# A reordered plan of 1325 calls in an attention and PReLU-FFN kernel, with three operations moved to other engines

## The chip, the cores and the metric

The kernel runs on one core of a Trainium2 chip. The metric is the device time of one execution in microseconds (us), and the number given for a kernel is the median of several executions. The engines are TensorE (PE in the profile, with its weight loads shown apart as PEld), VectorE (DVE), ScalarE (ACT), GpSimd (POOL) and SyncE (SP, which only issues DMAs here).

## What is computed

Attention with normalised queries and keys feeds a two-layer network with a PReLU between the layers. q, k and v are (8, 12, 448, 64): batch, heads, sequence, head size. The weights of the network are 768 x 2048 and 2048 x 768, and alpha has 2048 slopes.

```python
q_n, k_n = rmsnorm(q, g_q), rmsnorm(k, g_k)     # x / sqrt(mean(x*x) + 1e-6) * g
attn = softmax(q_n @ k_n.T / sqrt(64))          # 448 x 448 for each of 8 x 12 heads
x = (attn @ v), heads side by side              # 3584 x 768
h = x @ w_in                                    # 3584 x 2048
g = maximum(h, 0) + alpha * minimum(h, 0)
out = g @ w_out                                 # 3584 x 768, float32
```

## The kernel before

**Tiles.** The 96 heads are worked in 24 groups y of four heads; three groups make a batch b (0 to 7). The hidden layer is worked in 16 blocks ft of 128 columns for each batch. The output has 28 tiles of 128 rows, in two halves of 384 columns (OH). Tiles 0 to 5 are plain products (`down`). From tile 6 on, tiles go in pairs, and each pair is made from seven half-depth products instead of eight (`qa1` to `qc2`, and `quad` for the pairs 22, 24 and 26), with sums of weight blocks made beforehand (`mix_weights`) and sums of activations made for each pair (`mix_two` for two of them, then `mix_rest` for the other two).

**The plan.** One string, `PLAN`, names 1325 calls in one total order, and a loop at the end of the kernel carries them out in that order. The schedule is manual: each engine runs the instructions that it gets in the order in which the plan issues them, and waits by semaphores for what other engines have to deliver. So the plan sets the order within each engine. A call that changes its place only against calls of other engines changes nothing.

```python
for step in PLAN.split():
    ...
    acts[name](*given)
```

**A group's path.** `load_qk` (issued on SP) brings q and k. `square` (L370 on POOL, L368 on ACT) and `reduce` (L392, L401 on DVE) form the sums of squares, `fold` adds them up, `root` (L422, L423 on ACT) takes the inverse root, `scale` (L430 for groups from 9 on, L442 for earlier ones; on POOL from group 4 on unless an engine is named) applies it. `turn` transposes on PE (L568) up to group 8; after that `flip` (DVE) does, and `weigh` (L549, ACT) applies the gains. `score` (L596, PE) fills a PSUM tile with scores, `soft` (L610, ACT) takes the exponential. `den`, or `den_pre` with two copies on DVE, and `attend` (L621, PE) are the sums over keys; `log` or `log_pre` (L669) and `invert` (L679) on ACT turn the denominators over, and `times` (L717, DVE) writes the normalised result, xT.

**A block's path.** `up` (L734, PE) computes hT; `slope` (L775 on ACT, or L770 on DVE where the plan says `vec`) writes alpha * h and `larger` (L781, DVE) the maximum of the two, gT. `down` (L801) and `down_end` (L812, a copy on DVE and a store), or the products (L863) with their additions on DVE (`qa1v` at L879, `qa2v` L887, `qb1v` L905, `qc1v` L926, `quad`'s own around L996), end it. `mix_weights` is L831, `mix_two` L851 and L852, `mix_rest` L859: on POOL, save for one piece of `mix_weights`, (2,3), on DVE.

**What a product or score waits for.** Its data, and a PSUM tile. The pools are small: two tiles `sc` and one `acc` of two banks each, and two tiles `mm` of one bank. A further argument of `score`, `up`, `down`, `den`, `attend` or of a product chooses the pool, so a PE call often waits until ACT or DVE has read out the tile that it gets. In SBUF, three buffers hold the exponentials (`expT`); `mix_two(22)` takes one of these for its sums, `mix_two(20)` three of the four `nat` buffers of loaded q and k.

Of the kernel before, what the change touches and what calls it, by code (L numbers as in the profile page):

```python
# [39 lines left out]
invert(0+1) score(2,1,0) score(2,3,1) scale(3,q) load_w_in(2,4,8) soft(2,6) soft(2,2) times(0+1,1,0)  # L40
soft(2,1) times(0+1,1,1) soft(2,3) square(4,k) score(2,5,0) soft(2,5) square(5,k,act) times(0+1,0,0)
turn(3) den(2,1) attend(2,0,1) score(3,0,1) log(2) reduce(4,k,None) load_w_out(2) score(3,1,0)
square(4,q) load_w_in(3,0,4) invert(2) soft(3,1) begin(1) soft(3,0) times(2,0,0) begin(0)
square(5,q,act) up(0,0,0) reduce(4,q,None) up(0,1,0) slope(0,0) slope(0,1,vec) load_qk(6) root(4)
begin(3) begin(2) scale(4,q) score(3,5,0) up(0,4,0) larger(0,0) reduce(5,k) larger(0,1)
load_w_out(0) load_qk(7) reduce(5,q) slope(0,4) up(0,2,0) larger(0,4) slope(0,3) slope(0,2)
up(0,5,0) larger(0,3) scale(4,k) up(0,6,0) slope(0,5,vec) load_w_out(1) score(3,2,0) soft(3,5)
score(3,3,0) larger(0,2) square(6,q) slope(0,6) soft(3,3) soft(3,2) larger(0,5) turn(4) up(0,8,0)
score(4,0,1) soft(4,0) score(4,3,0) up(0,3,1) larger(0,6) score(4,1,0) soft(4,3) up(0,9,0) up(0,7,1)
up(0,11,0) slope(0,8,vec) square(6,k) larger(0,8) root(5) score(3,4,0) score(4,6,0) slope(0,9)  # L50
scale(5,k) reduce(6,q) up(0,13,0) larger(0,9) soft(4,1) slope(0,7) scale(5,q) soft(3,4)
slope(0,11,vec) larger(0,11) up(0,10,0) larger(0,7) square(7,q) soft(4,6) up(0,12,1) score(3,6,0)
slope(0,13) slope(0,10,vec) score(4,2,0) load_v(1) slope(0,12) larger(0,10) soft(4,2) larger(0,13)
up(0,14,0) larger(0,12) reduce(6,k) square(7,k,act) turn(5) slope(0,14) up(0,15,0) score(5,4,1)
soft(3,6) load_qk(8) root(6) larger(0,14) slope(0,15,vec) reduce(7,k) score(4,4,0) score(5,2,0)
larger(0,15) soft(5,4) scale(6,q,vec) down(1,0,0) soft(5,2) score(4,5,0) soft(4,4) soft(4,5)
scale(6,k,vec) load_w_out(3) score(5,0,1) square(8,q,act) reduce(7,q) soft(5,0) score(5,1,0)
down(0,0,0) reduce(8,q) square(8,k,act) turn(6) den(3+4,1) attend(3+4,0,0) score(5,5,0) score(5,6,0)
soft(5,1) mix_weights(0,1) log(3+4) invert(3+4) soft(5,5) soft(5,6) mix_weights(0,3) attend(3+4,1,0)
score(6,0,1) score(5,3,0) soft(6,0) score(6,4,0) down_end(0,0) down(2,0,0) soft(5,3) root(7)  # L60
scale(7,q) load_qk(9) soft(6,4) scale(7,k) den(5,0) attend(5,0,1) down_end(1,0) mix_weights(0,2)
times(3+4,0,0) times(3+4,1,0) times(3+4,1,1) load_qk(10) log(5) down(0,1,0) reduce(8,k) invert(5)
down_end(2,0) times(5,0,1) times(5,0,0) times(5,0,3) times(5,0,2) score(6,5,1) mix_weights(0,0)
score(6,1,0) down_end(0,1) score(6,6,0) soft(6,5) turn(7) up(1,1,1) square(9,q) down(1,1,0) root(8)
reduce(9,q) soft(6,6) score(6,3,1) score(7,0,0) slope(1,1) score(6,2,0) up(1,2,0) up(1,0,0)
soft(6,1) soft(7,0) soft(6,3) square(9,k) up(1,3,1) up(1,4,0) slope(1,2) slope(1,0) larger(1,1)
down_end(1,1) reduce(9,k) root(9) larger(1,2) load_qk(11) larger(1,0) slope(1,3) scale(8,q)
soft(6,2) up(1,7,0) slope(1,4) larger(1,3) larger(1,4) scale(8,k) score(7,4,0) slope(1,7)
larger(1,7) up(1,5,1) scale(9,q) turn(8) score(7,5,0) soft(7,4) score(7,1,0) up(1,6,0) square(10,q)
slope(1,5) larger(1,5) up(1,10,0) soft(7,5) soft(7,1) up(1,8,1) scale(9,k) up(1,9,0) reduce(10,q)  # L70
score(7,2,0) slope(1,6) slope(1,10) larger(1,6) mix_weights(1,1) score(7,6,0) slope(1,8) slope(1,9)
soft(7,6) up(1,12,1) up(1,11,0) soft(7,2) square(10,k) up(1,13,0) larger(1,8) larger(1,10)
slope(1,12) score(7,3,0) larger(1,9) up(1,14,1) slope(1,11) slope(1,13) mix_weights(1,3)
reduce(10,k) up(1,15,0) load_v(2) soft(7,3) larger(1,12) load_qk(12) score(8,3,0) score(8,0,0)
den(6+7,0) slope(1,14) fold(10) root(10) slope(1,15) soft(8,0) down(2,1,0) larger(1,11) larger(1,13)
square(11,q) log(6+7) score(8,1,0) score(8,4,0) soft(8,3) flip(9,k) scale(10,q) larger(1,14)
larger(1,15) score(8,5,1) mix_weights(3,1) down_end(2,1) reduce(11,q) square(11,k) weigh(9)
soft(8,5) down(3,0,0) soft(8,1) scale(10,k) score(8,2,0) flip(9,q) reduce(11,k) score(8,6,0)
soft(8,4) fold(11) load_qk(13) attend(6+7,0,0) attend(6+7,1,0) score(9,1,0) score(9,0,0)
down_end(3,0) soft(8,2) invert(6+7) score(9,2,1) down(3,1,0) times(6+7,0,0) soft(8,6) root(11)  # L80
times(6+7,1,0) load_qk(14) flip(10,q) down(4,0,1) mix_weights(1,2) soft(9,0) times(6+7,1,1)
score(9,5,0) square(12,q) soft(9,1) soft(9,2) scale(11,q) score(9,3,0) square(12,k) reduce(12,q)
down_end(3,1) soft(9,5) mix_weights(3,2) flip(10,k) scale(11,k) down_end(4,0) den_pre(8)
reduce(12,k) soft(9,3) attend(8,0,0) log_pre(8) score(9,6,0) fold(12) invert(8) root(12)
score(9,4,0) weigh(10) times(8,0,3) down(5,1,0) soft(9,4) times(8,0,1) times(8,0,0) flip(11,q)
down(4,1,0) score(10,0,0) soft(9,6) score(10,3,1) down_end(5,1) times(8,0,2) soft(10,0) soft(10,3)
score(10,2,0) up(2,0,0) up(2,1,0) slope(2,0) score(10,6,0) score(10,1,1) up(2,7,0) up(2,2,0)
down_end(4,1) up(2,4,1) slope(2,1) flip(11,k) soft(10,2) soft(10,1) slope(2,7) up(2,3,0)
mix_weights(2,0) slope(2,2) larger(2,0) scale(12,q) soft(10,6) slope(2,4) up(2,6,0) scale(12,k)
up(2,8,1) larger(2,1) slope(2,3) mix_weights(2,3) mix_weights(1,0) larger(2,7) square(13,k)  # L90
larger(2,2) up(2,10,0) square(13,q) up(2,5,0) larger(2,4) weigh(11) up(2,12,1) larger(2,3)
slope(2,6) up(2,14,0) slope(2,8) reduce(13,q) score(10,5,0) slope(2,10) mix_weights(2,2) load_v(3)
slope(2,5) slope(2,12) slope(2,14) score(10,4,0) soft(10,4) square(14,q) up(2,9,1) up(2,13,0)
soft(10,5) slope(2,13) larger(2,6) larger(2,8) larger(2,10) reduce(13,k) up(2,11,0) larger(2,5)
larger(2,12) load_qk(15) score(11,0,0) fold(13) den(9+10,1) slope(2,11) mix_weights(3,3) qa1(6,0)
up(2,15,0) qa2(6,1) root(13) mix_weights(3,0) flip(12,q) slope(2,9) larger(2,14) larger(2,13)
down(5,0,0) log(9+10) slope(2,15) larger(2,11) larger(2,9) invert(9+10) soft(11,0) square(14,k)
flip(12,k) reduce(14,q) weigh(12) qa1v(6) larger(2,15) mix_weights(2,1) scale(13,q) score(11,3,1)
scale(13,k) score(11,4,0) attend(9+10,0,1) mix_two(6,pool) soft(11,4) qa2v(6) mix_rest(6)
score(11,1,0) down_end(5,0) times(9+10,0,0) soft(11,3) square(15,q) reduce(14,k) attend(9+10,1,0)  # L100
score(12,0,0) soft(11,1) times(9+10,1,0) score(11,2,0) qa3(6,1) qb1(6,0) soft(11,2) fold(14) qa3v(6)
score(11,5,0) times(9+10,1,1) score(11,6,1) score(12,1,0) soft(12,0) soft(11,6) qb2(6,0) qc1(6,1)
qb1v(6) score(12,3,0) flip(13,k) soft(11,5) qb2v(6) qc1v(6) soft(12,1) den_pre(11) root(14)
soft(12,3) flip(13,q) score(12,2,1) attend(11,0,1) soft(12,2) mix_two(8,pool) score(12,6,1) qa1(8,0)
scale(14,q) log_pre(11) qc2(6,0) invert(11) times(11,0,0) qa2(8,1) weigh(13) times(11,0,3) qa3(8,0)
# [1007 lines left out]
```

## Time and profile before

| what | before |
|---|---|
| median of 3 runs | 407.5 us (407.3, 407.5, 408.99) |
| profiled execution | 407.36 us |
| its span | 405.6 us |
| mean granted TensorE clock | 0.99 |
| POOL, ACT, DVE busy | 70%, 68%, 67% of the span |
| DMA packets | 37173, 58.39 MB |

In the rows, L and a number is the line of the kernel; a row gives the operation, the tile written <- the tiles read, and partitions x elements with the type. In views in order of time a row begins with its start and its duration in us, "x4" counts like instructions that follow one another, and a bracket at the end gives the idle time of the engine just before and what ended it. In views by group the two numbers behind the bar are the busy time in us and the mean duration of one in ns.

### The profile page before, as it was taken

The page shows a single profiled execution, that of the slowest core. Times are in us where ns is not written, and L with a number is a line of the kernel's source. Part 1 is how long each engine was busy: PE and PEld are TensorE (multiplying, and loading weights), DVE is VectorE, ACT ScalarE, POOL GpSimd, SP SyncE. Part 2 cuts the span into 40 slices and gives each one's busy share as a digit, 9 for nine tenths or more (in the row PEclk, how much of TensorE's full clock was granted, in tenths as well). Part 3 has the DMA queues.
Part 4 walks back from the last instruction along what each step waited for, and adds up shares of the span by engine and source line. Part 5 has one row for each costly group of instructions (what it writes and reads, how often), then busy time and mean ns, then how long its engine had stood idle before and what let it go on. Part 6 is the DMA issues. An engine that isn't in the chain of part 4 may idle for free.

```text
span 405.6 us, 11966 instructions
## 1 busy us (share of the span) xinstructions
PE 390.8 (96%) x5071; PEld 208.5 (51%) x5071; DVE 271.6 (67%) x486; ACT 274.3 (68%) x409; POOL 283.3 (70%) x187
## 2 busy tenths in 40 slices
...
GB/s 273 222 263 237 222 252 118 236 209 169 110 163 174 183 162 145 104 187 187 229 121 91 128 229 167 143 220 108 114 41 137 11 3 22 60 79 0 31 108 98
DMA packets 37173, 58.39 MB, mean 144 GB/s; under 512 B 4720, under 2 KB 28928, under 8 KB 37120
## 3 DMA queue, kind: packets, MB, share of 16 engines
...
q8 instruction: 39, 0.64, 0.6%
...
## 4 chain that ended last, share of the span: by engine, by line
PE 89%; DVE 3%; ACT 2%; DMA 2%; POOL 1%; issue 1%; SPq 1%; POOLq 0%; DVEq 0%
PE hT L734 25%; PE hTa L734 10%; PE sc L596 8%; PE op L801 7%; PE qx L863 5%; PE av L621 5%; PE qz L863 4%; PE qc L863 4%; PE oq L863 4%; PE qxa L863 3%; PE dn L621 2%; PE avb L621 2%; DMA arena<-in_k_dram 2%; PE oqm L863 2%; PE qza L863 1%; PE oqa L863 1%
## 5 line engine op out<-in xcount | busy, mean ns | idle before, releaser
L610 ACT ACTIVATE expT<-sc 128x896 f16<-128x896 f32 x168 | 146.2, 916 | 41.5 <-PE sc L596 39.8
L734 PE MATMUL hT<-xT,w_in_sb 128*128 128x448 f16 x552 | 114.7, 353 | 0.5 <-DVE xT L717 0.5
L734 PEld LDWEIGHTS <-w_in_sb 128*128 128x128 f16 x768 | 73.1, 98 | 73.4 <-issue 8.7
L430 POOL TENSOR_TENSOR qs<-nat,rr 128x896 f16<-128x896 f32 x30 | 65.6, 2218 | 24.2 <-ACT rr L423 21.1
L781 DVE TENSOR_TENSOR gT<-hT,gT 128x448 f16<-128x448 f32 x92 | 56.7, 620 | 35.6 <-ACT gT L775 34.9
L775 ACT ACTIVATE gT<-hT,cols 128x448 f16<-128x448 f32 x86 | 54.5, 634 | 36.8 <-PE hT L734 35.8
L370 POOL TENSOR_TENSOR nat<-nat 128x896 f32<-128x896 f32 (+1 forms) x38 | 62.5, 1652 | 11.4 <-DVE gT L781 6.1
L596 PE MATMUL sc<-qT,kT 64*32 64x448 f16 (+1 forms) x1092 | 50.0, 359 | 5.7 <-ACT expT L610 4.2
L863 PEld LDWEIGHTS <-gT 128*128 128x128 f16 x352 | 33.4, 98 | 25.5 <-issue 3.8
L734 PE MATMUL hTa<-xT,w_in_sb 128*128 128x448 f16 x204 | 44.2, 353 | 0.0
L717 DVE TENSOR_TENSOR xT<-av,rden 64x448 f16<-64x448 f32 (+1 forms) x37 | 27.2, 736 | 11.7 <-ACT rden L679 4.6
L596 PEld LDWEIGHTS <-kT 64*32 64x32 f16 (+1 forms) x1092 | 16.8, 94 | 33.9 <-issue 25.7
L851 POOL TENSOR_TENSOR gs<-gT 128x1024 f16<-128x1024 f16 x4 | 8.5, 2124 | 36.7 <-DVE gT L781 36.7
L392 DVE TENSOR_REDUCE sp<-nat 128x28 f32<-128x896 f32 x30 | 32.1, 1070 | 2.0 <-DMA nat<-in_k_dram 2.0
L801 PE MATMUL op<-w_out_sb,gT 128*128 128x384 f16 x176 | 30.3, 326 | 0.2 <-DVE xT L717 0.2
L775 ACT ACTIVATE gT<-hTa,cols 128x448 f16<-128x448 f32 x34 | 21.6, 635 | 12.0 <-PE hTa L734 11.5
L781 DVE TENSOR_TENSOR gT<-hTa,gT 128x448 f16<-128x448 f32 x34 | 21.1, 619 | 10.6 <-ACT gT L775 10.2
L801 PEld LDWEIGHTS <-gT 128*128 128x128 f16 x192 | 18.3, 98 | 14.5 <-issue 3.0
L621 PEld LDWEIGHTS <-vt 64*32 64x32 f16 x1344 | 19.5, 92 | 12.0 <-issue 2.1
L621 PE MATMUL av<-expT,vt 64*32 64x448 f16 x896 | 24.3, 350 | 0.0
L859 POOL TENSOR_TENSOR gT<-gT 128x1024 f16<-128x1024 f16 x11 | 23.5, 2132 | 0.0
L863 PEld LDWEIGHTS <-arena 128*128 128x128 f16 x136 | 12.7, 98 | 10.5 <-issue 2.3
(151 smaller groups left out, 548.2 us busy)
## 6 DMA issues: line engine op xcount, KB each, us to landing
...
```

Of the source, the lines that this page charges most:

```text
L370: (eng or nc.gpsimd).tensor_mul(out=out, in0=src, in1=src)
L392: nc.vector.tensor_reduce(out=parts[y][:, ts("qk".index(nm), 4 * J), :1], in_=sqs[y, nm], axis=AXIS_X, op=ALU.add,)
L430: eng.tensor_mul(out=t.rearrange("p j d n -> p n j d"), in0=nat[y, nm][:, :, :HD].rearrange("p (n j) d -> p n j d", j=J), in1=r.unsqueeze( ...
L596: nc.tensor.matmul(out=sc[ds(64 * g + m * c, m), par, :S].rearrange("p (j c) -> p j c", j=J), lhsT=kT[ds(64 * par, 64), j, g, ts(c, m)], r ...
L610: nc.scalar.activation(out=expT[y][:, j], in_=scs[y, j][:, :, :S], func=AF.Exp, scale=QK_SCALE, bias=EXP_BIAS,)
L621: nc.tensor.matmul(out=accs[g][ds(32 * n, 32), :S], lhsT=weights(g, y, par, c, j), rhs=expT[y][ds(64 * g, 64), j, par, :], start=(j == 0), ...
L717: nc.vector.tensor_mul(out=o, in0=p, in1=q)
L734: nc.tensor.matmul(out=hT[:, :S], lhsT=w_in_sb[:, block_of(g, i), ts(ft, 128)], rhs=xT[b][:, g, i, :], start=(i == 0 and g == 0), stop=(i ...
L775: nc.scalar.activation(out=g, in_=hT[:, :S], func=AF.Copy, scale=alpha_sb[:, ft : ft + 1])
L781: nc.vector.tensor_max(out=g, in0=hT[:, :S], in1=g)
L801: nc.tensor.matmul(out=op[:, :OH], lhsT=gT[:, ft, ts(tile % J, 128)], rhs=w_out_sb[:, ft, ts(oh, OH)], start=(ft == 0), stop=(ft == NF - 1),)
L863: nc.tensor.matmul(out=bank[:, c], lhsT=g[:, ft], rhs=v[:, ft, c], start=(first and ft == 0), stop=(ft == HF - 1), skip_group_check=True,)
```

## The change

The change has two parts: the order of the plan from its 65th call on, and four calls whose engine or whose PSUM pool changes.

**The order.** Of 1325 calls 883 have another place, 58 of them by more than six places. The largest moves: mix_weights(1,3) 37 places earlier, mix_rest(18) 35 later, scale(17,q) 31 later, root(5) 28 earlier, scale(17,k) 26 earlier, load_qk(20) 25 later, mix_weights(3,0) 19 earlier, load_qk(18) 18 earlier. PE runs the same 428 calls with neighbours exchanged here and there. The exchanges within an engine that the prediction speaks of are these, each line with the calls of one engine in the plan's order, others left out:

```
- DVE   slope(0,5,vec) larger(0,2) larger(0,5) | turn(4) on PE
+ DVE   larger(0,2) slope(0,5,vec) larger(0,5) | turn(4) on PE
- DVE   down_end(2,0) times(5,0,1) times(5,0,0) times(5,0,3) times(5,0,2)
+ DVE   times(5,0,3) times(5,0,0) times(5,0,2) down_end(2,0) times(5,0,1)
- ACT   log_pre(11) invert(11) weigh(13)
+ ACT   weigh(13) log_pre(11) invert(11)
- DVE   times(14,0,3) times(14,0,2) qb1v(10) times(14,0,1) times(14,0,0)
+ DVE   times(14,0,3) times(14,0,1) times(14,0,2) qb1v(10) times(14,0,0)
- DVE   qc1v(12) larger(5,0) reduce(21,q) larger(5,1)
+ DVE   reduce(21,q) qc1v(12) larger(5,0) larger(5,1)
- DVE   larger(2,0) larger(2,1) mix_weights(2,3) larger(2,7)
+ DVE   mix_weights(2,3) larger(2,0) larger(2,1) larger(2,7)
- POOL  mix_two(20) mix_rest(20) mix_two(22) mix_rest(22)
+ POOL  mix_two(20) mix_two(22) mix_rest(20) mix_rest(22)
```

score(3,0) moves too, from before begin(1) to behind begin(2) and score(3,5,0).

**Engines and pools.** `square(22,q)` becomes `square(22,q,act)`, from POOL to ACT. `scale(13,q)` becomes `scale(13,q,vec)`, from POOL to DVE, and stands behind qa1v(6) and ahead of larger(2,15) there. `mix_rest(26)` becomes `mix_rest(26,vec)`, from POOL to DVE, for which the function gets an argument. `score(3,0,1)` and `score(17,5,1)` become `score(3,0,0)` and `score(17,5,0)`: from the one `acc` tile to one of the two `sc` tiles. `mix_weights` gets an argument for its engine too, which no call uses.

```diff
-    def mix_weights(n, p):
+    def mix_weights(n, p, eng=None):
...
-        eng = nc.vector if (n, p) in ((2, 3),) else nc.gpsimd
+        eng = eng or (nc.vector if (n, p) in ((2, 3),) else nc.gpsimd)
...
-    def mix_rest(tile):
+    def mix_rest(tile, eng=nc.gpsimd):
...
-            nc.gpsimd.tensor_sub(out=o, in0=a, in1=b)
+            eng.tensor_sub(out=o, in0=a, in1=b)
```

More of the change, by code (lines that the diff above doesn't have):

```diff
@@ L40 @@
[L40 to L105, printed above, removed]
@@ L124 @@
-soft(15,3) times(12+13,1,0) fold(17) den_pre(14) qa3v(10) root(17) attend(14,0,1) score(15,1,0)
-log_pre(14) score(16,0,1) invert(14) soft(15,1) mix_rest(10) times(14,0,3) qb1(10,0) times(14,0,2)
-qb2(10,0) qb1v(10) times(14,0,1) qc2(10,0) score(15,5,0) load_qk(20) score(15,4,1) soft(16,0)
-score(16,3,0) scale(17,q) qc1(10,0) soft(15,5) soft(16,3) score(15,6,0) times(14,0,0) score(16,2,0)
-up(4,2,0) up(4,4,1) qb2v(10) soft(15,4) square(18,k) soft(16,2) slope(4,2) up(4,1,0) square(18,q)
-qc2v(10) reduce(18,q) up(4,7,0) soft(15,6) qc1v(10) slope(4,4) slope(4,1) score(16,1,0) reduce(18,k)
@@ L142 @@
-score(18,0,0) soft(18,0) reduce(20,k) times(15+16,1,1) score(18,1,0) qb1v(12) fold(20) load_qk(21)
-larger(4,14) qb2(12,1) soft(18,1) scale(19,k) larger(4,15) score(18,3,0) soft(18,3) qb2v(12)
-den_pre(17) square(21,q) attend(17,0,1) flip(19,q) load_v(6) score(18,6,0) flip(19,k) score(18,2,1)
-log_pre(17) qc1(12,0) invert(17) times(17,0,0) times(17,0,1) times(17,0,3) times(17,0,2) soft(18,2)
-qc2(12,1) up(5,0,0) up(5,1,1) root(20) scale(20,q) scale(20,k) square(21,k) qc2v(12) soft(18,6)
-up(5,3,0) slope(5,0) up(5,2,0) weigh(19) score(18,4,0) slope(5,1) qc1v(12) score(18,5,1) load_qk(22)
@@ L178 @@
-larger(6,14) slope(6,15) attend(21+22,1,0) larger(6,15) log(21+22) invert(21+22) score(23,4,0)
-score(23,1,0) mix_two(20,pool,nat) times(21+22,0,0) qa2v(18) qa3v(18) qb1v(18) soft(23,5) qa1v(20)
-qb2(18,1) soft(23,2) qa2(20,0) times(21+22,1,0) soft(23,3) qc2(18,0) soft(23,1) times(21+22,1,1)
-qb2v(18) mix_rest(20) qa2v(20) qc2v(18) mix_two(22,pool,expT) soft(23,4) score(23,6,0) soft(23,6)
-mix_rest(22) attend(23,0,1) den_pre(23) log_pre(23) qa3(20,1) qb1(20,0) qb2(20,0) qa3v(20)
-invert(23) times(23,0,1) qc1(20,1) qb1v(20) qc1(18,0) times(23,0,3) times(23,0,0) qc2(20,0)
@@ L190 @@
-larger(7,14) larger(7,13) mix_two(24,pool,expT) mix_rest(24) mix_two(26,pool,expT) quad(22,1,0)
-quad(24,0,0) mix_rest(26) quad(26,1,1)
+soft(0,2) scale(2,q) soft(0,5) score(1,3,0) soft(1,1) turn(2) load_w_in(1,0,4) follow(2,q)
+score(1,2,0) soft(1,0) load_qk(4) square(3,k,pool,2) score(1,5,1) soft(1,4) reduce(3,k,0+1)
+soft(1,6) spin(2,0) soft(1,3) square(3,q) soft(1,2) slopes() soft(1,5) score(2,0,0) reduce(3,q,None)
+den(0+1,1) load_w_in(2,0,4) load_w_in(0,4,8) soft(2,0) score(2,4,1) root(3) log(0+1) attend(0+1,1,0)
@@ new lines @@
+flip(10,k) soft(9,0) down(4,0,1) times(6+7,1,1) soft(9,1) score(9,5,0) square(12,q) soft(9,2)
+square(12,k) score(9,3,0) scale(11,q) down_end(3,1) down_end(4,0) reduce(12,q) mix_weights(3,2)
+reduce(12,k) soft(9,5) soft(9,3) den_pre(8) attend(8,0,0) scale(11,k) score(9,6,0) log_pre(8)
+fold(12) score(9,4,0) invert(8) weigh(10) root(12) times(8,0,0) soft(9,4) times(8,0,3) down(5,1,0)
+flip(11,q) times(8,0,1) down(4,1,0) soft(9,6) score(10,0,0) score(10,3,1) times(8,0,2) soft(10,0)
+soft(10,3) up(2,0,0) up(2,1,0) score(10,2,0) slope(2,0) down_end(5,1) score(10,6,0) score(10,1,1)
@@ new lines @@
+mix_weights(3,0) larger(2,6) slope(2,13) larger(2,8) up(2,9,1) larger(2,10) reduce(13,k) up(2,11,0)
+larger(2,5) load_qk(15) larger(2,12) score(11,0,0) mix_weights(3,3) fold(13) den(9+10,1) qa1(6,0)
+up(2,15,0) qa2(6,1) root(13) slope(2,11) larger(2,14) larger(2,13) down(5,0,0) flip(12,q)
+larger(2,11) slope(2,9) slope(2,15) square(14,k) larger(2,9) soft(11,0) flip(12,k) mix_weights(2,1)
+reduce(14,q) qa1v(6) scale(13,q,vec) weigh(12) score(11,3,1) larger(2,15) scale(13,k) log(9+10)
+score(11,4,0) invert(9+10) soft(11,4) qa2v(6) attend(9+10,0,1) mix_two(6,pool) mix_rest(6)
@@ new lines @@
+score(11,1,0) soft(11,3) down_end(5,0) times(9+10,0,0) reduce(14,k) attend(9+10,1,0) score(12,0,0)
+soft(11,1) score(11,2,0) times(9+10,1,0) soft(11,2) qa3(6,1) qb1(6,0) fold(14) qa3v(6) square(15,q)
+score(11,5,0) times(9+10,1,1) score(11,6,1) score(12,1,0) qb2(6,0) soft(12,0) soft(11,6) qc1(6,1)
+score(12,3,0) qb1v(6) flip(13,k) soft(11,5) qb2v(6) qc1v(6) root(14) soft(12,1) den_pre(11)
+soft(12,3) mix_two(8,pool) flip(13,q) score(12,2,1) attend(11,0,1) soft(12,2) scale(14,q)
+score(12,6,1) qa1(8,0) qc2(6,0) qa2(8,1) weigh(13) log_pre(11) invert(11) times(11,0,3)
@@ new lines @@
+soft(15,3) load_qk(19) times(12+13,1,0) fold(17) root(17) den_pre(14) attend(14,0,1) qa3v(10)
+score(15,1,0) score(16,0,1) qb1(10,0) mix_rest(10) log_pre(14) invert(14) times(14,0,3) soft(15,1)
+qb2(10,0) times(14,0,1) qc2(10,0) times(14,0,2) score(15,5,0) score(15,4,1) soft(16,0) score(16,3,0)
+qc1(10,0) soft(15,5) soft(16,3) score(15,6,0) square(18,q) square(18,k) qb1v(10) times(14,0,0)
+score(16,2,0) up(4,2,0) up(4,4,1) qb2v(10) soft(15,4) scale(17,k) up(4,1,0) soft(16,2) slope(4,2)
+qc2v(10) up(4,7,0) reduce(18,q) soft(15,6) slope(4,4) qc1v(10) load_qk(20) score(16,1,0) slope(4,1)
@@ new lines @@
+qb1(12,1) up(4,14,0) slope(4,14) score(18,0,0) soft(18,0) score(18,1,0) times(15+16,1,1) fold(20)
+qb1v(12) load_qk(21) larger(4,14) soft(18,1) qb2(12,1) scale(19,q) larger(4,15) score(18,3,0)
+soft(18,3) qb2v(12) scale(19,k) den_pre(17) log_pre(17) square(21,q) attend(17,0,1) flip(19,q)
+load_v(6) score(18,6,0) flip(19,k) score(18,2,1) qc1(12,0) invert(17) times(17,0,1) times(17,0,2)
+times(17,0,0) soft(18,2) times(17,0,3) qc2(12,1) up(5,0,0) root(20) scale(20,q) up(5,1,1)
+scale(20,k) soft(18,6) square(21,k) qc2v(12) slope(5,0) up(5,3,0) up(5,2,0) slope(5,1) reduce(21,q)
@@ new lines @@
+reduce(22,k) qa2(16,0) qa1(16,0) score(20,3,1) weigh(21) larger(5,14) fold(22) soft(20,2) soft(20,5)
+larger(5,12) score(20,1,0) flip(21,q) attend(18+19,0,1) mix_two(16,pool) qa1v(16) attend(18+19,1,0)
+score(20,4,0) log(18+19) score(20,6,0) qa2v(16) invert(18+19) times(18+19,0,0) times(18+19,1,0)
+qa3(16,1) soft(20,1) qb1(16,0) root(22) soft(20,3) score(21,0,1) scale(22,k) soft(20,4)
+times(18+19,1,1) qc1(14,0) score(21,5,0) qa3v(16) soft(21,0) score(21,2,1) reduce(23,q) soft(20,6)
+soft(21,5) score(21,3,0) qb1v(16) qc1v(14) soft(21,2) den_pre(20) log_pre(20) attend(20,0,1)
```

187 lines of the change are left out of this document (116 added, 71 removed).

## The prediction

> **What bounds the kernel now.** I read the page's header and part 1 first, then busy time by stretch (start:end, length, then busy time and instruction count of PE, PEld, DVE, ACT, POOL, then the granted TensorE clock, DMA share, GB/s), then the instructions in order of time round each place where the plan differs.
>
> ```profile
> span 405.6 us, 11966 instructions
> ...
> PE 390.8 (96%) x5071; PEld 208.5 (51%) x5071; DVE 271.6 (67%) x486; ACT 274.3 (68%) x409; POOL 283.3 (70%) x187
> ```
>
> ```profile
> 11.90:18.70 6.80, 4.18 (x34) 2.21 (x34) 5.86 (x9) 6.74 (x12) 3.38 (x6) 0.50 1.12 241
> 18.70:25.50 6.80, 5.11 (x97) 2.88 (x105) 5.24 (x9) 6.46 (x9) 3.98 (x5) 1.00 1.16 273
> 25.50:32.30 6.80, 6.06 (x169) 2.78 (x146) 5.14 (x7) 6.43 (x10) 4.59 (x10) 1.00 1.10 238
> ...
> 40.00:80.00 40.00, 39.37 (x544) 20.63 (x543) 31.21 (x47) 29.25 (x44) 23.73 (x18) 1.00 1.04 203
> 80.00:240.00 160.00, 159.83 (x2136) 83.49 (x2134) 114.89 (x216) 120.83 (x180) 137.87 (x77) 1.00 0.71 162
> 240.00:400.00 160.00, 159.82 (x1912) 87.96 (x1911) 96.78 (x179) 90.30 (x134) 94.93 (x49) 1.00 0.38 86
> ```
>
> TensorE (PE) is the bound: 405.6 - 390.8 = 14.8 us of idle in the whole span, and from 80 to 400 only 0.17 + 0.18 = 0.35. The matmuls stay the same 428 PE calls in almost the same order. So the change can give back at most PE's waits behind the 65th call (which runs at about 21 us): 1.69 + 0.74 between 18.7 and 32.3, where ACT is busy 6.4 to 6.5 of each 6.8 and is itself the limit, 0.63 from 40 to 80, 0.35 later. It can cost wherever a swap makes a producer later than its slack, that is later than the PE call that reads it. After 80 there is nearly no wait left in which such a delay could be absorbed: each goes to the end nearly whole.
>
> **The change part by part.** The moves reorder each engine's own queue in places (some 30 swaps each on ACT and DVE, 15 on POOL); a call that only changes its place among calls of other engines moves nothing. I went through every swap and compared the delay of what falls behind with the slack of its reader.
>
> ```profile
> 44.56 0.67 DVE L770 TENSOR_SCALAR gT<-hT,cols 128x448 f16<-128x448 f32 x1
> 45.15 0.61 DVE L781 TENSOR_TENSOR gT<-hTb,gT 128x448 f16<-128x448 f32 x1
> 45.82 0.94 PE L568 MATMUL tps<-ident,qs 128*128 128x128 f16 x14 [0.24 <-DVE gT L781]
> ```
>
> A, -0.24. turn(4) waits 0.24 for larger(0,2), which stands behind the 0.67 of slope(0,5,vec). The new order puts larger(0,2) first: the wait goes. The score(3,0) that changes its PSUM bank and moves behind begin(2) is in this stretch too; before shows it only in its old place, so -0.3 to +0.3 round nothing; likewise score(17,5), which changes its bank.
>
> ```profile
> 76.25 0.56 DVE L812 COPY osb<-op 128x384 f32<-128x384 f32 x1 [1.33 <-PE op L801]
> ...
> 78.47 2.53 DVE L717 TENSOR_TENSOR xT<-av,rden 64x448 f16<-64x448 f32 x4 [1.67 <-PE av L621]
> ...
> 80.97 0.76 PE L596 MATMUL sc<-qT,kT 64*64 64x448 f16 x12
> ```
>
> B, +0.2. down_end(2,0)'s copy (0.56) moves from a DVE gap into the four times(5,0,*): their end goes from 81.00 to 81.56. The third score of the x12 row (start 80.97 + 2 x 0.2 = 81.37) takes the bank that they free.
>
> ```profile
> 172.22 0.58 ACT L679 ACTIVATE rden<-rden 128x448 f32<-128x448 f32 x1
> 172.70 1.03 ACT L549 ACTIVATE kT<-kT,gain 128x896 f16<-128x896 f16 x1
> ...
> 172.83 1.26 DVE L717 TENSOR_TENSOR xT<-av,rden 64x448 f16<-64x448 f32 x2 [0.98 <-ACT rden L679]
> ...
> 176.29 0.56 DVE L887 TENSOR_TENSOR osb<-qxa,osb 128x384 f32<-128x384 f32 x1 [0.37 <-PE qxa L863]
> 176.88 0.62 DVE L717 TENSOR_TENSOR xT<-av,rden 64x448 f16<-64x448 f32 x1
> ...
> 177.49 0.76 PE L596 MATMUL sc<-qT,kT 64*32 64x448 f16 x24
> ```
>
> C, +0.4, the largest. weigh(13) (1.03) is put ahead of log_pre(11) and invert(11); the DVE waits for that invert before times(11,0,*). They start about 0.97 later; 0.37 of it is absorbed where the DVE waits for PE before qa2v. The last times ends at 177.50 and the second score of the x24 row (177.49 + 0.2) takes its bank, a slack of 0.19: 0.97 - 0.37 - 0.19 = 0.41.
>
> ```profile
> 218.08 0.56 DVE L905 TENSOR_TENSOR osb<-qz,osb 128x384 f32<-128x384 f32 x1
> ...
> 219.03 1.46 PE L863 MATMUL qc<-w_out_sb,s 128*128 128x384 f16 x8
> ```
>
> D, +0.25. One times(14,0,1), half of a 1.26 row like that under C or 0.63, now stands ahead of qb1v(10), whose end at 218.64 frees the bank of qc2(10) at 219.03: 0.63 - 0.39.
>
> ```profile
> 261.69 0.55 DVE L926 TENSOR_TENSOR osb<-qc,osb 128x384 f32<-128x384 f32 x1
> ...
> 263.17 2.05 PE L734 MATMUL hT<-xT,w_in_sb 128*128 128x448 f16 x10
> 263.50 1.08 DVE L392 TENSOR_REDUCE sp<-nat 128x28 f32<-128x896 f32 x1
> ```
>
> E, +0.1. reduce(21,q), 1.08, now goes ahead of qc1v(12), which frees the bank of up(5,3,0): slack 263.17 - 262.24 = 0.93. The other thirty swaps have more slack than what is put ahead, or nearly: reduce(19,k) among the larger calls of b = 4 and reduce(12,*) ahead of den_pre(8) are the tight ones. I allow +0.25 for all of them (0 to +0.6).
>
> Then the edits that change an engine, all costed at nothing:
>
> ```profile
> 135.29 0.62 DVE L781 TENSOR_TENSOR gT<-hT,gT 128x448 f16<-128x448 f32 x1 [1.39 <-ACT gT L775]
> 136.94 1.21 DVE L831 TENSOR_TENSOR w_out_sb<-w_out_sb 128x768 f16<-128x768 f16 x1
> ...
> 275.85 0.64 ACT L775 ACTIVATE gT<-hT,cols 128x448 f16<-128x448 f32 x1 [2.29 <-PE hT L734]
> ```
>
> ```profile
> L442 DVE TENSOR_TENSOR qs<-nat,rr 128x896 f16<-128x896 f32 x2 | 2.1, 1083 | 0.0
> ...
> L368 ACT ACTIVATE nat<-nat 128x896 f32<-128x896 f32 x3 | 2.8, 945 | 0.2 <-DMA nat<-in_q_dram 0.2
> ```
>
> square(22,q) on ACT costs 0.945 there and fits the 2.29 that ACT waits for PE before 275.85; without that cover it costs up to 0.95. scale(13,q) on DVE takes about 1.08 by the L442 row; the larger(2,15) behind it is late by 0.4 to 0.5, and qa3(6), the next PE reader behind it, has over 1 us; without the cover 0.5. mix_weights(2,3), an order change, moves into the 1.39 in which the DVE waits before 135.29.
>
> ```profile
> 391.99 2.12 POOL L859 TENSOR_TENSOR gT<-gT 128x1024 f16<-128x1024 f16 x1
> ...
> 392.63 0.56 DVE L996 TENSOR_TENSOR osb<-oqm,osb 128x384 f32<-128x384 f32 x1 [0.74 <-PE oqm L863]
> 395.03 2.76 PE L863 MATMUL oq<-w_out_sb,gT 128*128 128x384 f16 x16
> ```
>
> mix_rest(26) ends on POOL at 394.11; its reader is the second half of the x16 row, 395.03 + 8 x 0.163 = 396.33. On DVE it has to wait behind quad(24)'s last add (end 393.19). The nearest DVE row of the kind is mix_weights, 1.21 for 768 columns, so at most 1.61 each for 1024 and 3.2 for both: end 396.4, +0.1; at half of that, 394.8, nothing. A gain is excluded, as POOL's result was there 2.2 us early. I take nothing, and 0 to +0.2.
>
> ```profile
> 223.16 1.72 SPq L326 DMA_DIRECT2D nat<-in_k_dram  x4
> ...
> 242.44 1.68 POOL L370 TENSOR_TENSOR nat<-nat 128x896 f32<-128x896 f32 x1 [2.23 <-DVE gT L781]
> ```
>
> On SP's queue load_qk(20) goes 25 places down and past two sends, load_qk(18) 18 up. The loads of that time are issued at 223.16 and before, and POOL's square reads y = 20 at 242.44: 17 us of cover, so nothing.
>
> Sum: -0.24 + 0.2 + 0.4 + 0.25 + 0.1 + 0.25 = +0.96 on the span, 406.6. The profiled execution took 407.36, 1.76 more than its span: 408.3; the median of the runs shown, 407.5, lies 0.14 higher, so I give **408.4**.
>
> One rule speaks against the moved mix_weights(2,3). In before it ran beside POOL:
>
> ```profile
> 136.10 1.63 POOL L831 TENSOR_TENSOR arena<-w_out_sb,arena 128x768 f16<-128x768 f16 x1
> ...
> 137.70 3.62 POOL L370 TENSOR_TENSOR nat<-nat 128x896 f32<-128x896 f32 x2
> ```
>
> It started at 136.94 and ended at 138.15, 0.42 after POOL's operation ended (137.73). The Trainium skill, "SBUF — State Buffer", section "Who interferes with whom", says that a VectorE operation with two SBUF operands and a GpSimd operation shut each other out, the later one waiting whole. The trace fits it. By it the sum would be the same if the slot at 134 is free, and 1.2 more if POOL takes the lock first: that is a rival.
>
> **The rivals.** (1) The swaps change nothing: each delay is eaten by slack that I read too small, as ends of matmuls are modelled; 407.5 (406.9 to 407.9). For it: every term is a few tenths. Against: the banks in B, C and D are handed on within 0.4.
> (2) Small gain: half of PE's waits from 18.7 to 400 (2.43 + 0.63 + 0.35 = 3.4) goes and no new one comes: 407.5 - 1.1 = 406.4, with about 0.4 either way. Against: ACT is the limit in the larger half.
> (3) Clear gain: nearly all of 18.7 to 80 goes, 407.5 - 2.6 = 404.9.
> (4) POOL first: mix_weights(2,3) can start only when POOL's next operation is done, as it was seen to end 0.42 after POOL; larger(2,0) then starts at about 136.7 and not 135.29, up(2,7) behind it is 1.2 late: 408.4 + 1.2 = 409.6.
>
> ```profile
> 340.01 1.51 PE L621 MATMUL avb<-expT,vt 64*32 64x448 f16 x56
> ...
> 346.04 1.61 PE L621 MATMUL av<-expT,vt 64*32 64x448 f16 x56
> ...
> 350.86 1.46 PE L863 MATMUL qz<-w_out_sb,gT 128*128 128x384 f16 x8
> ```
>
> (5) On the other side, the chain on POOL at tiles 20 and 22. mix_two(22), two operations of about 2.12 like mix_rest's, is now ahead of mix_rest(20), another two, and needs the buffer of an earlier group. Freed by the attend at 340.01, it runs 341.6 to 346, and mix_rest(20) ends at 350.1, 0.7 before qb2(20) at 350.86: nothing. Freed only by the attend that ends at 347.6, mix_rest(20) ends at 347.6 + 8.5 = 356.1 and PE waits 5.2: 408.4 + 5.2 = 413.6. It decides from the point where mix_rest(20) ends after 350.86; against it speaks that the order of the buffers gives the first.
> (6) Half clock. From 11.9 to 18.7 the granted clock was 0.50, right behind a stretch with many idle gaps. If the same befell 25.5 to 32.3 because a gap before it grows, half of 6.8, 3.4, would be done in it where 6.06 is done now, 2.7 less: 408.4 + 2.7 = 411.1. The Trainium skill, "TensorE: Matmul & The Clock Gate", section "🔬 Part 1: The HAM clock gate", ties the clock to the activity of the window before; the trace agrees with its 0.50 row.
>
> **How the numbers follow.** Chances: forecast 408.4 (its own range 407.4 to 409.4) 0.45; (1) 0.22; (2) 0.10; (3) 0.06; (4) 0.07; (5) 0.06; (6) 0.03; anything else that is slower 0.01. The range 406.0 to 409.8 leaves out (3), (5), (6) and the rest, 0.16. 0.5% is 2.04 us, about what a measurement of this kernel can tell from no change: faster, below 405.46, is (3), 0.06; slower, above 409.54, is (4), (5), (6) and the rest, 0.17; the same 0.77.
>
> **What would show it.** A: no wait before the turn(4) at 45.6. B, C, D: PE waits of some tenths named after L717 or L905 at about 81, 178 and 219. POOL: mix_rest(20) ends before qb2(20). The end: oq x16 without a wait for DVE L859. PE's idle from 80 to 400 should rise from 0.35 to about 1.5 us. It is wrong if that idle stays below 0.6, or if a single wait over 1 us appears.

## The result and the profile after

The changed kernel takes 409.52 us in the median of 10 runs (408.44 to 412.42), the kernel before 407.16 in 10 runs (406.71 to 408.99): the medians lie 2.36 us apart. The ratio of the runs, by which the kernels below are compared too, is 1.0049 with a 95% interval of 1.0032 to 1.0067: slower by about 2.0 us (1.3 to 2.7). One later run of the changed kernel, at 414.44 us, was in a slower state and is in no ratio below. The profiled execution took 410.18 us, with a span of 408.4.

The lines of the changed kernel are one lower than in before (L734 is L733). First the page's header and part 1 of the changed kernel, and its busy time by stretch, with the columns of the prediction's table:

```profile
span 408.4 us, 11974 instructions
...
PE 396.4 (97%) x5071; PEld 209.6 (51%) x5071; DVE 274.4 (67%) x489; ACT 275.1 (67%) x410; POOL 275.6 (67%) x183
```

```profile
11.90:18.70 6.80, 5.19 (x44) 2.32 (x42) 6.54 (x9) 6.55 (x12) 4.12 (x7) 0.50 1.11 238
18.70:25.50 6.80, 5.86 (x45) 2.49 (x44) 5.04 (x8) 5.63 (x8) 3.71 (x5) 0.50 1.16 268
25.50:32.30 6.80, 6.69 (x190) 3.05 (x190) 4.85 (x8) 5.96 (x10) 5.28 (x10) 0.88 1.10 227
...
80.00:240.00 160.00, 159.60 (x2104) 83.15 (x2109) 116.86 (x219) 119.08 (x178) 132.67 (x74) 1.00 0.72 165
240.00:400.00 160.00, 159.72 (x1940) 87.03 (x1925) 97.59 (x180) 92.57 (x137) 91.27 (x47) 1.00 0.37 83
```

Two things are to be seen. PE's idle time from 80 to 400 is 0.40 + 0.28 = 0.68, up from 0.35 and far less than the 1.5 that the prediction looked for, though the kernel is slower. And the half clock, which lasted for one stretch in before, lasts for two and a little more here. Both mislead when taken alone. The waits are mostly hidden from the idle time, as the next rows show, and the half clock comes and goes without the change, as the point on rival (6) shows.

What shows the loss is the lag of PE's calls: the start of a call here less its start in before, taken only where the same calls have been issued up to then. It falls or grows in steps, and each step names a place. These rows of the changed kernel, in order of time, are where the prediction expected steps:

```profile
46.14 0.61 PE L595 MATMUL sc<-qT,kT 64*64 64x448 f16 x8
46.68 0.95 PE L567 MATMUL tps<-ident,qs 128*128 128x128 f16 x14
...
82.24 0.95 PE L595 MATMUL sc<-qT,kT 64*64 64x448 f16 x12
...
179.06 0.98 PE L595 MATMUL sc<-qT,kT 64*32 64x448 f16 x24
...
221.22 1.46 PE L862 MATMUL qc<-w_out_sb,s 128*128 128x384 f16 x8
...
265.56 1.67 PE L733 MATMUL hT<-xT,w_in_sb 128*128 128x448 f16 x8
```

The bracket of a wait is gone from turn(4) at 46.68 (A). The twelve score matmuls of B span 0.95 where they spanned 0.76, the 24 of C 0.98 where 0.76: the waits lie inside a row of like instructions, which the profile folds together, and since it models the ends of matmuls, a stalled matmul counts as busy there. So a stall of 0.1 to 0.3 us shows as a longer row or a later start, not as idle time. That is why the idle time rose by only a third of a microsecond.

On DVE and ACT the same places read:

```profile
173.20 1.03 ACT L548 ACTIVATE kT<-kT,gain 128x896 f16<-128x896 f16 x1
174.13 0.57 ACT L668 ACTIVATE rden<-rden 128x448 f32<-128x448 f32 x1
174.73 0.58 ACT L678 ACTIVATE rden<-rden 128x448 f32<-128x448 f32 x1
```

```profile
175.34 1.26 DVE L716 TENSOR_TENSOR xT<-av,rden 64x448 f16<-64x448 f32 x2 [1.91 <-ACT rden L678]
...
178.80 0.62 DVE L716 TENSOR_TENSOR xT<-av,rden 64x448 f16<-64x448 f32 x1
...
218.68 1.90 DVE L716 TENSOR_TENSOR xT<-av,rden 64x448 f16<-64x448 f32 x3 [0.79 <-ACT rden L678]
220.61 0.56 DVE L904 TENSOR_TENSOR osb<-qz,osb 128x384 f32<-128x384 f32 x1
...
263.96 1.07 DVE L391 TENSOR_REDUCE sp<-nat 128x28 f32<-128x896 f32 x1
264.95 0.55 DVE L925 TENSOR_TENSOR osb<-qc,osb 128x384 f32<-128x384 f32 x1
...
352.76 1.26 DVE L716 TENSOR_TENSOR xT<-av,rden 64x448 f16<-64x448 f32 x2 [1.31 <-ACT rden L678]
354.06 0.56 DVE L895 TENSOR_TENSOR osb<-qxa,osb 128x384 f32<-128x384 f32 x1
...
356.94 0.54 DVE L917 TENSOR_TENSOR osb<-qz,osb 128x384 f32<-128x384 f32 x1
```

C: the DVE's wait for the inversion grew from 0.98 to 1.91, by the 0.93 that weigh(13) now takes ahead of it. D: three operations of `times` in a row, then qb1v(10), which ends at 221.17, and qc2(10) starts at 221.22. E: reduce(21,q), then qc1v(12), which ends at 265.50, and up(5,3) starts at 265.56. The last three rows belong to a swap that the prediction had not priced by itself: at tile 20 two times(23,0,*) now stand ahead of qa3v(20), and they wait for an inversion, so the DVE stands still for 1.31 with qa3v behind it. On PE, qc1(20) takes the bank that qa3v(20) frees, and qc2(20) the one that the second addition of qb2v(20) (L917) frees. DVE and PE in before:

```profile
349.75 0.56 DVE L896 TENSOR_TENSOR osb<-qxa,osb 128x384 f32<-128x384 f32 x1 [0.70 <-PE qxa L863]
...
354.04 0.55 DVE L918 TENSOR_TENSOR osb<-qz,osb 128x384 f32<-128x384 f32 x1
```

```profile
352.15 1.46 PE L863 MATMUL qca<-arena,gT 128*128 128x384 f16 x8
...
354.75 1.46 PE L863 MATMUL qc<-w_out_sb,gs 128*128 128x384 f16 x8
```

The same two products in the changed kernel:

```profile
354.67 1.46 PE L862 MATMUL qca<-arena,gT 128*128 128x384 f16 x8
...
357.53 1.46 PE L862 MATMUL qc<-w_out_sb,gs 128*128 128x384 f16 x8
```

In before the banks were free 1.84 and 0.16 ahead of the two products. In the changed kernel both products start 0.05 behind the addition that frees their bank.

### The profile page after: what moved, and what is told of

It is laid out like the page before. It is cut to its first block, busy times and chain, and to the rows that moved or that the text cites. A ratio compares the mean times of both kernels' runs of the same rounds, so it can differ in the third digit from the quotient of the medians.

```text
span 408.4 us, 11974 instructions
## 1 busy us (share of the span) xinstructions
PE 396.4 (97%) x5071; PEld 209.6 (51%) x5071; DVE 274.4 (67%) x489; ACT 275.1 (67%) x410; POOL 275.6 (67%) x183
## 5 line engine op out<-in xcount | busy, mean ns | idle before, releaser
L733 PE MATMUL hT<-xT,w_in_sb 128*128 128x448 f16 x552 | 114.8, 353 | 0.2 <-DVE xT L716 0.2
L733 PEld LDWEIGHTS <-w_in_sb 128*128 128x128 f16 x768 | 73.0, 98 | 73.2 <-issue 8.9
L429 POOL TENSOR_TENSOR qs<-nat,rr 128x896 f16<-128x896 f32 x29 | 63.5, 2228 | 22.0 <-ACT rr L422 21.4
L369 POOL TENSOR_TENSOR nat<-nat 128x896 f32<-128x896 f32 (+1 forms) x37 | 60.5, 1642 | 21.2 <-DMA nat<-in_q_dram 12.6
L595 PE MATMUL sc<-qT,kT 64*32 64x448 f16 (+1 forms) x1092 | 52.1, 367 | 3.2 <-ACT expT L609 2.3
L733 PE MATMUL hTa<-xT,w_in_sb 128*128 128x448 f16 x204 | 44.2, 353 | 0.0
L716 DVE TENSOR_TENSOR xT<-av,rden 64x448 f16<-64x448 f32 (+1 forms) x37 | 27.2, 736 | 17.1 <-ACT rden L678 7.6
L595 PEld LDWEIGHTS <-kT 64*32 64x32 f16 (+1 forms) x1092 | 17.1, 95 | 32.8 <-issue 24.5
L858 POOL TENSOR_TENSOR gT<-gT 128x1024 f16<-128x1024 f16 x10 | 21.3, 2128 | 0.0
L850 POOL TENSOR_TENSOR arena<-gT 128x1024 f16<-128x1024 f16 x7 | 15.0, 2136 | 9.0 <-DVE gT L780 9.0
```

The lines of the kernel that those rows point to most:

```text
L369: (eng or nc.gpsimd).tensor_mul(out=out, in0=src, in1=src)
L429: eng.tensor_mul(out=t.rearrange("p j d n -> p n j d"), in0=nat[y, nm][:, :, :HD].rearrange("p (n j) d -> p n j d", j=J), in1=r.unsqueeze( ...
L595: nc.tensor.matmul(out=sc[ds(64 * g + m * c, m), par, :S].rearrange("p (j c) -> p j c", j=J), lhsT=kT[ds(64 * par, 64), j, g, ts(c, m)], r ...
L716: nc.vector.tensor_mul(out=o, in0=p, in1=q)
L733: nc.tensor.matmul(out=hT[:, :S], lhsT=w_in_sb[:, block_of(g, i), ts(ft, 128)], rhs=xT[b][:, g, i, :], start=(i == 0 and g == 0), stop=(i ...
```

## The experiments

A lag to 0.1 us can be read from one profile, while the medians settle some 0.15%. So each kernel below was both timed and traced. The ratios are to runs of before on the same chip: before took 408.01 beside the first four kernels, 408.10 beside the last four. Lags are to the one trace of before.

### The changed kernel again

No edit.

> The changed kernel once more, to see what belongs to the plan and what to one execution. Theory of the swaps: the lag of its matmuls behind those of before grows again by 1.9 us between 48 us and the end, at the same calls, whatever the first 48 us did; of this the 0.44 inside attend(3+4,1,0) may not come back, which would leave about 1.5. Rival, the clock: the changed kernel draws more half-clock time at the start (17 us of it in the profile shown, against 6.7 in before), and its time follows the granted clock from run to run: runs with a mean clock of 0.99 are as fast as before, those at 0.98 are 2 us and more slower.

Measured: 409.81 us in 11 runs, ratio 1.0044 (1.0028 to 1.006). The lag grew by 1.45 us between 48 us and the end, at the same calls and by nearly the same steps as in the first trace, save one: the 0.44 inside attend(3+4,1,0) came back neither here nor in any later trace, so it belongs to that one execution. The clock rival fell, since the loss is there at an equal clock. Above 0.985 the two runs of the changed kernel (408.31 and 410.69) took 409.5 in the mean, and seven of before 407.7. Up to 0.979 four runs took 410.4, and ten of before 408.2.

### The new order only up to 57 us

```
plan: calls 1 to 209 of the changed kernel, then calls 210 to 1325 of the kernel before
```

> The new order for the first 209 calls (to about 57 us) and the old order, engines and pools behind them. Theory of the swaps: as fast as before or 0.3 us faster, from the wait of turn(4) that goes. Rival, the clock: all of the slowdown is here, +2 us, with a lower mean clock than before's.

Measured: 407.96 us, ratio 0.9998 (0.9987 to 1.0008). The step at turn(4) is -0.28 in its lag, and none that lasts comes behind it. The early part does not cost the 2 us.

### The new order only behind 57 us

```
plan: calls 1 to 209 of the kernel before, then calls 210 to 1325 of the changed kernel
```

> The old order for the first 209 calls, the new order, engines and pools behind them. Theory of the swaps: slower than before by 1.5 to 1.9 us, the lag growing at score(6,1), down(5,1), score(13,0), qc2(10), up(5,3) and at tile 20. Rival, the clock: as fast as before.

Measured: 409.21 us, ratio 1.0033 (1.002 to 1.0046), 1.3 us, a little under the 1.5 to 1.9 that was expected; its lag grows by 1.45 behind 48 us. The loss is behind 57 us.

### Only the three operations on their new engines

```diff
- larger(2,15) mix_weights(2,1) scale(13,q) ... square(22,q) ... mix_rest(26)
+ larger(2,15) mix_weights(2,1) scale(13,q,vec) ... square(22,q,act) ... mix_rest(26,vec)
```

> The old order with only the three operations on their new engines: square(22,q) on ScalarE, scale(13,q) and mix_rest(26) on VectorE. Theory of the swaps: within 0.2 us of before, since each lies in a gap of its engine and its reader has slack. Rival, the engines: up to +0.5 from scale(13,q) in front of larger(2,15), +0.95 from the square, and more than 0.2 at the end if mix_rest(26) ends after 396.3 us.

Measured: 408.59 us, ratio 1.002 (1.0008 to 1.0032): the expectation missed. The lag grows by 0.40 at qb2(8), 0.1 at up(3,1) and 0.59 at up(3,3). The first operation of mix_two(6) on POOL, qb2(8) and up(3,3) in before:

```profile
157.25 2.12 POOL L851 TENSOR_TENSOR arena<-gT 128x1024 f16<-128x1024 f16 x1 [0.17 <-DVE gT L781]
```

```profile
181.22 1.47 PE L863 MATMUL qza<-w_out_sb,gT 128*128 128x384 f16 x8
...
185.94 2.43 PE L734 MATMUL hT<-xT,w_in_sb 128*128 128x448 f16 x12
```

DVE, POOL and PE of this kernel:

```profile
157.03 2.17 DVE L429 TENSOR_TENSOR qs<-nat,rr 128x896 f16<-128x896 f32 x1
```

```profile
157.19 3.80 POOL L850 TENSOR_TENSOR arena<-gT 128x1024 f16<-128x1024 f16 x1 [2.20 <-DVE gT L780]
161.07 2.14 POOL L851 TENSOR_TENSOR arena<-arena,gT 128x1024 f16<-128x1024 f16 x1
...
179.41 2.12 POOL L858 TENSOR_TENSOR gT<-gT 128x1024 f16<-128x1024 f16 x1
```

```profile
181.58 1.47 PE L862 MATMUL qza<-w_out_sb,gT 128*128 128x384 f16 x8 [0.33 <-POOL gT L858]
...
186.98 2.43 PE L733 MATMUL hT<-xT,w_in_sb 128*128 128x448 f16 x12 [0.42 <-DVE gT L780]
```

scale(13,q) takes 2.17 on DVE and not 1.08, and the first operation of mix_two(6), which started 0.16 later on POOL, took 3.80 where it took 2.12 in before. That fits a wait until the DVE was done, at 159.20, though not to the tenth: from there to the end of POOL's operation are 1.79 and not 2.12. POOL's queue is 1.6 late from there to mix_rest(8), which ends at 181.53, and PE waits for it at 181.58.

### Five swaps alone

```diff
- down_end(2,0) ... times(5,0,2)
+ down_end(2,0) times(5,0,2)
- log_pre(11) invert(11) ... weigh(13)
+ weigh(13) log_pre(11) invert(11)
- qb1v(10) times(14,0,1)
+ times(14,0,1) qb1v(10)
- qc1v(12) larger(5,0) reduce(21,q)
+ reduce(21,q) qc1v(12) larger(5,0)
- qa3v(20) invert(23) times(23,0,1) qb1v(20) times(23,0,3) times(23,0,0) times(23,0,2)
+ invert(23) times(23,0,2) times(23,0,1) qa3v(20) qb1v(20) times(23,0,3) times(23,0,0)
```

In the first pair down_end(2,0) moves down behind three times(5,0,*). The last pair changes the DVE's order by putting two times(23,0,*) ahead of qa3v(20); their inversion, on ACT, has to stand ahead of them.

> The old kernel with only five swaps: down_end(2,0) ahead of the last times(5,0,*), weigh(13) ahead of log_pre(11) and invert(11), times(14,0,1) ahead of qb1v(10), reduce(21,q) ahead of qc1v(12), and invert(23), times(23,0,2) and times(23,0,1) ahead of qa3v(20). Theory of the swaps: the lag of the matmuls behind those of before grows by 0.15, 0.2, 0.3, 0.1 and 0.4 us at score(6,1), score(13,0), qc2(10), up(5,3) and qc1(20) to qc2(20), and nowhere else; 1.1 to 1.2 us in all, 0.3% slower than before. Rival: the many other moves share the loss, and this kernel loses less than 0.6.

Measured: 409.69 us, ratio 1.0043 (1.0027 to 1.0059). The lag grows at the five places, by 0.18, 0.35, 0.30, 0.12 and 0.38, and nowhere else: 1.32 in all, behind 48 us. The rows of C in this kernel:

```profile
174.76 1.26 DVE L716 TENSOR_TENSOR xT<-av,rden 64x448 f16<-64x448 f32 x2 [1.91 <-ACT rden L678]
...
178.36 0.62 DVE L716 TENSOR_TENSOR xT<-av,rden 64x448 f16<-64x448 f32 x1
```

```profile
178.49 0.38 PE L595 MATMUL sc<-qT,kT 64*32 64x448 f16 x8
179.02 0.57 PE L595 MATMUL sc<-qT,kT 64*32 64x448 f16 x16 [0.15 <-DVE xT L716]
```

The last times ends at 178.98, and the second score starts at 179.02. These five swaps alone cost nearly as much as the whole change (1.32 of 1.45 in the lag).

### The changed kernel without the five

The five swaps are undone, the other moves, engines and pools stay.

> The changed kernel with the same five swaps undone, all else as changed. Theory of the swaps: the lag grows by no more than 0.3 us behind 48 us (0.13 at down(5,1), 0.1 at up(3,3), 0.07 at qa3(12)), and the time is within 0.3% of before. Rival: it stays 0.3 to 0.4% slower.

Measured: 408.58 us, ratio 1.0009 (0.9992 to 1.0025). The five steps are gone. Behind 48 us the lag still grows by 0.61, twice what was expected: 0.11 at up(1,1), 0.11 at down(5,1), 0.09 at qa3(12), and 0.30 at up(3,3). Which move makes the first three late was not looked into.

### The scaling ahead of larger(2,15)

```diff
- larger(2,15) mix_weights(2,1) scale(13,q,vec)
+ scale(13,q,vec) larger(2,15) mix_weights(2,1)
```

> The three operations on their new engines in the old order, as in the run before, but scale(13,q) stands ahead of larger(2,15) on VectorE, where the changed kernel has it, and not behind it. Theory of the blocked port: mix_two(6) then cannot begin beside the scaling, its first operation takes 2.1 us again and not 3.8, POOL ends mix_rest(8) about 0.9 us earlier than with the scaling behind, and PE's waits at qb2(8) and up(3,3) shrink from 0.36 and 0.7 us to under 0.2 in all; 0 to 0.2 us slower than before. Rival, the scaling is merely long (2.17 us on VectorE where 1.08 was assumed): larger(2,15) is 0.7 later, mix_two(6) too, and the waits stay.

Measured: 408.61 us, ratio 1.0014 (1.0 to 1.0028). The theory of the blocked port was right on POOL and at qb2(8): mix_two(6)'s first operation takes 2.13, and PE has no wait there. It was wrong on up(3,1) and up(3,3), which still come 0.1 and 0.59 late. Rows of this kernel on POOL, DVE and PE:

```profile
158.16 2.13 POOL L850 TENSOR_TENSOR arena<-gT 128x1024 f16<-128x1024 f16 x1 [3.49 <-DVE gT L780]
...
180.78 1.69 POOL L369 TENSOR_TENSOR nat<-nat 128x896 f32<-128x896 f32 x1
```

```profile
182.50 1.09 DVE L391 TENSOR_REDUCE sp<-nat 128x28 f32<-128x896 f32 x1 [0.70 <-POOL nat L369]
```

```profile
186.29 2.43 PE L733 MATMUL hT<-xT,w_in_sb 128*128 128x448 f16 x12 [0.43 <-DVE gT L780]
```

Here the scaling, 2.17 long, holds up larger(2,15), and with it mix_two(6), though POOL had been free for 3.49. POOL's queue is about 0.9 late again, and 1.3 against PE, whose calls come 0.38 earlier in this trace; square(15,k) at its end is late too, the DVE stands 0.70 in front of reduce(15,k), and a larger of b = 3 queued behind that frees up(3,3)'s bank late. So both theories hold a part: by this comparison the wait of POOL beside the scaling cost the 0.40 at qb2(8), the plain length of the scaling the rest.

### The early part, the square and mix_rest(26)

```
plan: calls 1 to 209 changed, the rest as before, with square(22,q,act) and mix_rest(26,vec); scale(13,q) on POOL
```

> The new order for the first 209 calls, the old order behind them, square(22,q) on ScalarE and mix_rest(26) on VectorE, scale(13,q) left on POOL. Theory of the swaps: no lag beyond 48 us, 0 to 0.3 us faster than before by the wait of turn(4); the two engine moves cost nothing. Rival: the square or mix_rest(26) costs 0.2 us or more.

Measured: 407.89 us, ratio 0.9991 (0.9974 to 1.0009). The only lasting step of the lag behind 40 us is -0.28 at turn(4). The two engine moves cost nothing. Its ratio is the lowest of all these kernels, but its gain of 0.2 to 0.3 us, as the lag has it, is below what the runs can tell from no change.

## Why the prediction was right, point by point

The range (406.0 to 409.8) held the time, but only at its upper end: 409.52 lies outside the forecast's own 407.4 to 409.4, and about +2.0 us came where +0.9 was forecast. That the range went so far it owes to rival (4), at 409.6, which did not come: that part is luck. What was right is the direction and the mechanism: swaps that make a producer later than its slack, each passed to the end nearly whole. The steps of the lag, in us, each read from the call ahead of the place to the call behind it:

| step | forecast | changed | again | five swaps | without the five |
|---|---|---|---|---|---|
| A, turn(4) | -0.24 | -0.28 | -0.28 | - | -0.28 |
| attend(3+4,1,0) | 0 | +0.41 | 0 | 0 | 0 |
| B, scores of y = 6 | +0.2 | +0.19 | +0.19 | +0.18 | 0 |
| up(1,1) | 0 | 0 | 0 | 0 | +0.11 |
| down(5,1) | in "other" | +0.11 | +0.11 | 0 | +0.11 |
| C, score(13,0) | +0.4 | +0.22 | +0.22 | +0.35 | 0 |
| up(3,3) | 0 | +0.10 | +0.07 | 0 | +0.30 |
| D, qc2(10) | +0.25 | +0.30 | +0.30 | +0.30 | 0 |
| qa3(12) | in "other" | +0.08 | +0.07 | 0 | +0.09 |
| E, up(5,3) | +0.1 | +0.12 | +0.11 | +0.12 | 0 |
| tile 20 | in "other" | +0.38 | +0.38 | +0.38 | 0 |
| all behind 48 us (without A) | +1.20 | +1.91 | +1.45 | +1.32 | +0.61 |

Of the 0.44 at attend(3+4,1,0), 0.03 is made up again by 80 us. From 40 us on, A included, the repeat's lag grows by 1.18, and the terms of the sum come to 0.96. Part of that closeness is two errors that offset each other, C too high by 0.2 and the other swaps too low by 0.3.

**A, B, D and E** came within 0.1. **C** is right when it stands alone (0.35 against 0.41). In the full change it is 0.22. There the DVE has qc2v(6) ahead of the third times(11,0,*) and not behind it, and gets from the start of the first to the end of the last in 4.08 (175.34 to 179.42) instead of 4.22 (174.76 to 178.98). C at score(13,0) and POOL's lateness at up(3,3) together make 0.29 to 0.32, and without C POOL's alone makes 0.30: two delays that overlap, not two that add.

**The other swaps** were under-sized: 0.25 against 0.56 to 0.57, of which tile 20 has 0.38. What failed in that step is the judgement that those left had "more slack than what is put ahead, or nearly". The swap at tile 20 put ahead of qa3v(20) two operations that were not yet ready. The price of such a swap is their 1.26 and the wait in front of them, another 1.31 for the inversion. So even the 1.84 of slack ahead of qc1(20) did not suffice, and in the full change this step is the largest of all that come again in the repeat.

**scale(13,q) at nothing** was wrong in size and in cover. The 1.08 came from a row at another line, L442, with the same partitions, elements and types; the call goes through L430, which writes 16-bit values in steps of four, and takes 2.17 on DVE (2.22 on POOL). To look at the slack of qa3(6) was to look at the wrong reader: larger(2,15) starts mix_two(6), and with it a queue on POOL that has hardly a gap up to square(15,k) at 182 us. The scaling ahead of it makes mix_two(6) wait 4.06 in the changed kernel, where the wait was 0.17 in before:

```profile
159.69 2.13 POOL L850 TENSOR_TENSOR arena<-gT 128x1024 f16<-128x1024 f16 x1 [4.06 <-DVE gT L780]
```

In before POOL spent 2.2 of that time on the scaling itself. Against PE, whose calls are 1.59 later here, mix_two(6) starts 0.85 later. In the changed order the move costs at most 0.3, in the old order 0.7 to 1.1. **The square** took 0.96 in its gap, as said. **mix_rest(26)** was bounded at 1.61 each and took 0.68 to 0.69 in both traces of the changed kernel, here one of its two operations in the repeat:

```profile
L858 DVE TENSOR_TENSOR gT<-gT 128x1024 f16<-128x1024 f16 x1 | 0.7, 685 | 0.0
```

**The idle time** was the wrong sign. It was to rise to about 1.5, with waits named at B, C and D, and to stay above 0.6. It rose to 0.68, and none of the three waits is named in the changed kernel's views, though the delays are there. That it passed 0.6 at all is no evidence. No single wait of PE over 1 us appears from 40 us to 400.

**The rivals.** No swallowing and no gain: (1) to (3) fell, as the intervals of the changed kernel, of the late order alone and of the five swaps alone lie above 1. Two sums of the prediction are off: half of the 3.4 in (2) is 1.7 and not 1.1, which gives 405.8, below the range; and the forecast's terms add up to 408.46, not 408.4. (4), the moved mix_weights(2,3) held up by POOL, did not come: in its new place it took 0.65, where it had taken 1.21 beside POOL's operation in before. In the repeat of the changed kernel:

```profile
133.65 0.65 DVE L830 TENSOR_TENSOR w_out_sb<-w_out_sb 128x768 f16<-128x768 f16 x1
135.12 0.62 DVE L780 TENSOR_TENSOR gT<-hT,gT 128x448 f16<-128x448 f32 x1 [0.82 <-ACT gT L774]
```

The mechanism behind (4) did show where it had not been looked for, in the 3.80 of mix_two(6) in the old order. That is what the Trainium skill says in "SBUF — State Buffer", "Who interferes with whom": the later of the two waits whole. The trace agrees nearly, as POOL lost 1.68 of the 2.01 us for which the DVE was still busy. In its new place the moved mix_weights(2,3) lost nothing. It started at 133.65 beside a pair of scalings on POOL, which took 4.50 instead of the 4.24 in before; the second of the pair, begun at 133.88, took that time longer, so here too it was the later one that waited.

(5), POOL's chain at tile 20, came out on the safe side and close. POOL and PE of the changed kernel:

```profile
344.25 2.13 POOL L850 TENSOR_TENSOR gs<-gT 128x1024 f16<-128x1024 f16 x1 [3.72 <-PE avb L620]
...
350.63 2.12 POOL L858 TENSOR_TENSOR gT<-gT 128x1024 f16<-128x1024 f16 x1
```

```profile
353.25 1.46 PE L862 MATMUL qz<-w_out_sb,gT 128*128 128x384 f16 x8
```

The attend of groups 21 and 22 freed the buffer, as forecast; mix_rest(20) ends at 352.75, 0.50 before qb2(20), where 0.7 was forecast. (6), the half clock, did befall the profiled execution, from 10 to 27 us. It is not the change's doing: it set in ahead of the first call that moved, at 21 us, and the kernel of the five swaps, whose calls are those of before up to 76 us, had it from 9.7 to 26.7 us in its trace. The 31 runs of before beside the repeat had mean clocks from 0.977 to 0.992 too. Its price is smaller than the 2.7 that the prediction gave for one stretch more: of these runs, the ten with a mean clock up to 0.979 took 408.2 in the mean and the seven above 0.985 took 407.7.

What stays open: the lag from 40 us on, A included, grew by 1.2 us in the repeat, where the two timings say 1.8 (1.1 to 2.4) and 2.0 (1.3 to 2.7). The larger part is shown. In the other kernels the timing lies on both sides of the lag from 40 us on: 1.3 against 1.4 for the late order, 0.8 against 1.1 for the three engines, 1.8 against 1.3 for the five swaps. Whether the rest is chance, or executions with stalls like the 0.44 at attend(3+4,1,0), of which the changed kernel's longer tail (up to 412.42, and once 414.44) may be a sign, was not settled.
